# GpSimd's upper part held behind VectorE's last operation of a step, and the second attention's stages one step earlier

## The chip, the cores and the metric

One core of one Trainium2 chip runs the kernel. The metric is the device time of one execution in microseconds, lower is better; the time of a kernel is the median of its runs.

## What is computed

Two set-attention blocks over 12480 tokens of 128 features with 32 inducing points, then two feed-forward blocks of width 2048, all in float32:

```python
def mab(q, kv):
    s = scale * (q @ kv.transpose(0, 2, 1))
    s = s - s.max(-1, keepdims=True)
    a = np.exp(s)
    a /= a.sum(-1, keepdims=True) + 1e-09
    return a @ kv
h = mab(I, x)                        # 32 inducing points look at all tokens
x = mab(x, h)                        # every token looks at the 32 results
h = x @ w_in;  x = (h * np.clip(h + 3.0, 0.0, 6.0) / 6.0) @ w_out      # first block
h = x @ w_in2; x = np.maximum(h, 0.0) ** 2 @ w_out2                    # second block
```

## The kernel before

The first attention (lines 260 to 442) gives 32 x 128 numbers and ends some 43 us into the span. Everything after it is the main loop at the end of the program, which the change touches.

The tokens are cut into 25 chunks of 512 columns, chunk 13 of 192 (`SHORT`). The width 2048 is cut into 8 pieces of two 128-row blocks, so a chunk has 8 steps; step k belongs to chunk c = k // 8, piece p = k % 8, and there are K = 200 steps and a tail of 14. Step k works on layer 1 of piece k and on layer 2 of piece j = k - 11, which belongs to an earlier chunk.

For layer 1, `up1` (L598, two matmuls into a PSUM tile h1) applies the attention's second product and the first weight at once: `m4` holds the inducing results times the weight, so the right operand is the chunk's attention weights `a_t`. `gate1` runs a Relu with bias on ScalarE (L606) and then min and product on VectorE (L607, SBUF and PSUM operands). The gated values g1 are split into two parts for the float32r matmuls: `high1` rounds them (hi1; GpSimd at L618, for a few early steps ScalarE), `low1` takes the rest, g1 - hi1, on VectorE (L626). `down1` (L646, six matmuls into yacc) follows two steps later. At a chunk's last piece yacc is written out as yh on ScalarE (L663) and yl on VectorE (L664); yacc has one buffer, so the next chunk's first down1 has to wait for both.

For layer 2, `up2` (L675, six matmuls), `relu2` and `square2` on ScalarE (L686, L690), `high2` (hi2, L700 on ScalarE) and `low2` (L706 on VectorE, both operands in SBUF) do the same, and `down2` (L646, six matmuls into oacc) follows three steps later; a chunk's oacc is copied by VectorE (L719) and stored. A step thus issues 2 + 6 + 6 + 6 = 20 matmuls. The h tiles of both layers and the scores share three PSUM buffers (pool `hp`).

The attention of the next chunk is spread over steps of the present one: `att_scores` (TensorE, L484) and `att_shift` (VectorE: transpose L504, maximum L507, subtraction L509) at p = 1, `att_exp` (ScalarE, L517) at p = 2, `att_norm` (VectorE: L524, L526, L530, L532 and a transpose back, L550) at p = 3, `att_upper` (ScalarE, ah, L570) at p = 4, `att_spread` at p = 5 (VectorE, al, L577, and 16 transfers of 16 KB from ah and al into a_t on the SP queue, L583). The a_t has two buffers.

What sets the order: until step KM = 24 a scheduler of the framework orders the instructions (there the weights are converted too, L173 to L217, on VectorE, GpSimd and ScalarE). From step 24 on (`tc.manual_schedule()`) each engine runs its instructions in the order in which the program issues them. There VectorE's order in a step is gate, low1 of the step before, low2; `high1` is issued behind the gate.

Of the kernel before, what the change touches and what calls it, by code (L numbers as in the profile page):

```python
# [10 lines left out]
F32 = mybir.dt.float32  # L11
F32R = mybir.dt.float32r
# [9 lines left out]
P = 128  # L22
# [42 lines left out]
L1, L2 = 2, 3  # L65
MIX = (0, 3)
PRE = 26
KM = 24
# [7 lines left out]
def induced_attention_then_two_ffn(  # L76
# [11 lines left out]
    nc = tc.nc  # L88
    NT, D = x.shape
    M = indT.shape[1]  # L90
# [19 lines left out]
    sel = const.tile([P, M], F32, name="sel")  # L110
    blk4 = const.tile([P, J], F32, name="blk4")
    three = const.tile([P, 1], F32, name="three")
    ind = const.tile([P, M], F32, name="ind")
    inds = const.tile([P, M], F32, name="inds")
    ht4 = const.tile([P, J, M], F32, name="ht4")
# [11 lines left out]
    def load_x(c):  # L127
        t = xpool.tile([P, size[c]], F32, tag="xc", name="xc")
        n = at_token[c]
        nc.sync.dma_start(t, xT[:, n:n + size[c]])  # L130
        x_of[c] = t
# [95 lines left out]
    def tick():  # L227
        n = len(ticks)
        ticks.append(n)
        for g in list(live):  # L230
            if next(g, live) is live:
                live.remove(g)
        for item, (when, cut_at, _) in PLAN.items():
            if when == n:
                load_until(item)
                live.append(convert(item))
                next(live[-1])
        for item, (when, cut_at, _) in PLAN.items():
            if cut_at == n:
                live.append(cut(item))  # L240
                next(live[-1])
# [18 lines left out]
    with ExitStack() as pro:  # L260
# [159 lines left out]
        for g in range(NG - 1):  # L420
            j = g % J
# [47 lines left out]
    def mix_low(q):  # L469
        t = m4[2 * M:, q * CW:(q + 1) * CW]  # L470
        nc.vector.tensor_tensor(out=t, in0=mixed.pop(q)[2 * M:, :], in1=t, op=ALU.subtract)
# [4 lines left out]
    def blocks(c):  # L476
        nb = J if size[c] == CH else 2
        return nb, size[c] // nb
# [17 lines left out]
    def att_shift(c):  # L496
        nb, n = blocks(c)
        s = att.pop(c)
        if c == 0:
            st = hp.tile([P, J, M], F32, tag="h", name="pst")  # L500
            nc.tensor.transpose(st.rearrange("p j i -> p (j i)"), s, ident)
        else:
            st = sp.tile([M * nb, n // M, M], F32, tag="st", name="st", bufs=1)
            nc.vector.transpose(st.rearrange("p b i -> p (b i)"), s)  # L504
        shape = list(st.shape)
        nm = sp.tile(shape[:2], F32, tag="nm", name="nm")
        nc.vector.tensor_reduce(out=nm, in_=st, axis=AX.X, op=ALU.max, negate=True)  # L507
        t = sp.tile(shape, F32, tag="t", name="t")
        nc.vector.tensor_tensor(  # L509
            out=t, in0=st, in1=nm.unsqueeze(2).to_broadcast(shape), op=ALU.add  # L510
        )
        att[c] = t

    def att_exp(c):
        t = att.pop(c)
        e = sp.tile(list(t.shape), F32, tag="e", name="e")
        nc.scalar.activation(e, t, AF.Exp, scale=SCALE)  # L517
        att[c] = e

    def att_weights(c):  # L520
        e = att.pop(c)
        shape = list(e.shape)
        l = sp.tile(shape[:2], F32, tag="l", name="l")
        nc.vector.tensor_reduce(out=l, in_=e, axis=AX.X, op=ALU.add)  # L524
        le = sp.tile(shape[:2], F32, tag="le", name="le")
        nc.vector.scalar_tensor_tensor(  # L526
            out=le, in0=l, scalar=EPS, in1=l, op0=ALU.add, op1=ALU.max
        )
        r = sp.tile(shape[:2], F32, tag="r", name="r")
        nc.vector.reciprocal(r, le)  # L530
        a = sp.tile(shape, F32, tag="a", name="a")
        nc.vector.tensor_tensor(  # L532
            out=a, in0=e, in1=r.unsqueeze(2).to_broadcast(shape), op=ALU.mult
        )
        return a

    def att_norm(c):
        a = att_weights(c)
        if c == 0:
            a4 = sp.tile([P, J, 2, 2, M], F32R, tag="a4", name="a4", bufs=1)  # L540
            nc.vector.tensor_copy(a4[:, :, 0, 0, :], a)
            nc.scalar.copy(a4[:, :, 1, 0, :], a)
            for k in range(2):
                last = nc.vector.tensor_tensor(
                    out=a4[:, :, k, 1, :], in0=a, in1=a4[:, :, 0, 0, :], op=ALU.subtract
                )
            att[c] = a4
            return last
        at = sp.tile([a.shape[0], a.shape[1] * M], F32, tag="aback", name="aback", bufs=1)
        nc.vector.transpose(at, a.rearrange("p b i -> p (b i)"))  # L550
        att[c] = at

    def att_turn(c):
        a4 = att.pop(c)
# [8 lines left out]
        return nc.scalar.copy(a_t[c], pt)  # L563


    def att_upper(c):
        nb, n = blocks(c)
        at = att.pop(c)
        ah = sp.tile([M * nb, n], F32R, tag="ah", name="ah", bufs=1)
        nc.scalar.copy(ah, at)  # L570
        att[c] = at, ah

    def att_spread(c):
        nb, n = blocks(c)
        at, ah = att.pop(c)
        al = sp.tile([M * nb, n], F32R, tag="al", name="al", bufs=1)
        nc.vector.tensor_tensor(out=al, in0=at, in1=ah, op=ALU.subtract)  # L577
        a_t[c] = sp.tile([P, size[c]], F32R, tag="at", name="at")
        for v, part in enumerate((ah, al)):
            for u in range(2):  # L580
                for b in range(nb):
                    to = M * (2 * u + v)
                    nc.sync.dma_start(  # L583
                        a_t[c][to:to + M, b * n:(b + 1) * n].bitcast(F32),
                        part[M * b:M * (b + 1), :].bitcast(F32),
                    )

    K = NCH * NP
    h1, g1, hi1, lo1 = {}, {}, {}, {}
# [137 lines left out]
    def on(f, k):  # L727
        if 0 <= k < K:
            f(k)
# [28 lines left out]
    for k in range(K + OFF + L2 + 1):  # L758
        if k == KM:
            behind.close()  # L760
            ctx.enter_context(tc.manual_schedule())
        c, p = divmod(k, NP)
        j = k - OFF
        on(up1, k)
        if k < KM:
            on(low1, k - 1)
        tick()
        on(gate1, k)
        on(high1, k)
        if k >= KM:  # L770
            on(low1, k - 1)
        on(square2, j - 1)
        on(up2, j)
        on(relu2, j)
        on(high2, j - 1)
        on(low2, j - 2)
        tick()
        if k in MIX:
            q = MIX.index(k) + 2
            mix(q)  # L780
            mix_high(q)
            mix_low(q)
        if c + 1 < NCH:
            if p == 0 and LAST < c + 2 < NCH:
                load_x(c + 2)
            if p == 1:
                att_scores(c + 1)
                att_shift(c + 1)
            if p == 2:
                att_exp(c + 1)  # L790
            if p == 3:
                att_norm(c + 1)
            if p == 4:
                att_upper(c + 1)
            if p == 5:
                att_spread(c + 1)
        on(down1, k - L1)
        on(down2, j - L2)


# [26 lines left out]
```

## Time and profile before

| | us |
|---|---|
| median of 3 runs | 1019.51 (1017.94 to 1025.77) |
| the profiled execution, its own time | 1021.25 |
| its span in the trace | 1019.1 |
| busy: TensorE / VectorE / ScalarE / GpSimd | 969.5 / 932.8 / 822.1 / 392.6 |

The span is the time from the first to the last recorded instruction; the execution's own time has 2.15 us around it. PE is TensorE's matmuls, PEld its weight loads, DVE VectorE, ACT ScalarE, POOL GpSimd, SP the engine that issues transfers. The ends of matmuls are modelled, so their starts tell the pace. A bracket behind a row gives the idle time of the engine before it and what ended it.

### The profile page before, as it was taken

Reading aid. Unit: us, or ns where it says so; the run is one execution under the profiler, and the core shown is the slowest. Engines: PE = TensorE matmul, PEld = TensorE weight load, DVE = VectorE, ACT = ScalarE, POOL = GpSimd, SP = SyncE. Lnnn points to the kernel's source line nnn. Section 1 sums busy time; section 2 is a strip of 40 time slices with the busy share of each in tenths; the row PEclk is TensorE's granted clock in tenths of the full one; section 3 lists DMA queues with packets and bytes.
Section 4 is the critical chain, followed back from the end, with each engine's and each line's share of the span. In section 5 each row is a group of like instructions: output and inputs, shape, how many; then the busy total and the mean of one; then the engine's idle time right before and its main releaser. Section 6 shows DMA issues by size and latency. Waiting matters only on the chain.

```text
span 1019.1 us, 12914 instructions
## 1 busy us (share of the span) xinstructions
PE 969.5 (95%) x4614; PEld 764.3 (75%) x4614; DVE 932.8 (92%) x956; ACT 822.1 (81%) x952; POOL 392.6 (39%) x241
## 2 busy tenths in 40 slices
PE   8777999999999999999999879999999999999998
PEld 6434787787787787787788768778778778778786
DVE  4898889999999999999997898999999999999974
ACT  6646898888888888888889757888888888888886
POOL 2465214343343343343451244334334334334323
PEclk9997999999999999999999999999999999999999
DMA  9521010010010010000000010011011011000000
GB/s 354 167 69 50 18 32 6 26 32 6 27 32 5 27 32 6 27 25 5 27 25 9 23 32 25 3 30 32 2 31 29 4 31 31 3 20 21 1 11 21
DMA packets 32879, 34.54 MB, mean 34 GB/s; under 512 B 7600, under 2 KB 25008, under 8 KB 32304
## 3 DMA queue, kind: packets, MB, share of 16 engines
q1 hardware_dynamic: 32816, 33.73, 10.5%
q8 instruction: 36, 0.59, 0.2%
q14 instruction: 27, 0.22, 0.1%
HBM read 21.18 MB, written 6.39 MB: 27 GB/s over the span
## 4 chain that ended last, share of the span: by engine, by line
DVE 58%; PE 27%; ACT 6%; DMA 4%; issue 3%; SPq 1%; POOL 1%; ACTq 0%; DVEq 0%; POOLq 0%
DVE lo L706 22%; DVE g L607 14%; DVE lo L626 13%; PE oacc L646 9%; PE yacc L646 8%; PE h L675 6%; ACT g L606 3%; PE h L598 3%; DMA at<-ah 2%; DVE yl L664 1%; ACT hi L700 1%; SPq L583 1%; ACT g L690 1%; DVE osb L719 1%; DMA raw<-in_w1a 1%
## 5 line engine op out<-in xcount | busy, mean ns | idle before, releaser
L618 POOL TENSOR_SCALAR hi<-g 128x1024 fp32r<-128x1024 f32 (+1 forms) x180 | 330.6, 1837 | 539.4 <-DVE g L607 539.4
L706 DVE TENSOR_TENSOR lo<-g,hi 128x1024 fp32r<-128x1024 f32 (+2 forms) x201 | 380.2, 1892 | 12.3 <-PE oacc L646 6.0
L606 ACT ACTIVATE g<-h,three 128x1024 f32<-128x1024 f32 (+1 forms) x200 | 219.2, 1097 | 143.1 <-PE h L598 142.7
L607 DVE SCALAR_TENSOR_TENSOR g<-g,h 128x1024 f32<-128x1024 f32 (+1 forms) x200 | 236.1, 1182 | 34.8 <-ACT g L606 34.4
L626 DVE TENSOR_TENSOR lo<-g,hi 128x1024 fp32r<-128x1024 f32 (+1 forms) x187 | 221.9, 1187 | 5.1 <-POOL hi L618 3.6
L690 ACT ACTIVATE g<-g 128x1024 f32<-128x1024 f32 (+2 forms) x201 | 206.0, 1026 | 0.4
L686 ACT ACTIVATE g<-h 128x1024 f32<-128x1024 f32 (+2 forms) x201 | 199.5, 993 | 6.8 <-PE h L675 6.7
L700 ACT CAST hi<-g 128x1024 fp32r<-128x1024 f32 (+2 forms) x188 | 191.6, 1020 | 0.0
L675 PE MATMUL h<-yh,wh 128*128 128x512 f32 (+1 forms) x400 | 155.2, 388 | 0.4 <-DVE g L607 0.2
L675 PE MATMUL h<-yh,wl 128*128 128x512 f32 (+1 forms) x400 | 154.3, 386 | 0.0
L675 PE MATMUL h<-yl,wh 128*128 128x512 f32 (+1 forms) x400 | 154.1, 385 | 0.0
L598 PE MATMUL h<-at,m 128*128 128x512 f32 (+1 forms) x400 | 129.7, 407 | 15.8 <-DMA at<-al 7.8
L646 PE MATMUL yacc<-hi,wh 128*128 128x512 f32 (+1 forms) x374 | 118.3, 397 | 18.1 <-DVE yl L664 18.1
L646 PE MATMUL oacc<-hi,wh 128*128 128x512 f32 (+1 forms) x400 | 123.9, 390 | 1.0 <-DVE osb L719 1.0
L646 PE MATMUL oacc<-hi,wl 128*128 128x512 f32 (+1 forms) x400 | 122.1, 386 | 0.0
L646 PE MATMUL oacc<-lo,wh 128*128 128x512 f32 (+1 forms) x400 | 122.0, 386 | 0.0
L646 PE MATMUL yacc<-hi,wl 128*128 128x512 f32 (+1 forms) x374 | 114.3, 387 | 0.0
L646 PE MATMUL yacc<-lo,wh 128*128 128x512 f32 (+1 forms) x374 | 114.0, 386 | 0.0
L598 PEld LDWEIGHTS h<-at,m 128*128 128x128 f32 x400 | 75.5, 193 | 39.3 <-issue 14.3
L646 PEld LDWEIGHTS yacc<-hi,wh 128*128 128x128 f32 x374 | 66.5, 188 | 41.7 <-issue 30.7
L646 PEld LDWEIGHTS oacc<-hi,wh 128*128 128x128 f32 x400 | 73.4, 189 | 22.1 <-issue 6.8
L675 PEld LDWEIGHTS h<-yh,wh 128*128 128x128 f32 x400 | 75.6, 189 | 17.7 <-ACT g L686 1.3
(114 smaller groups left out, 854.8 us busy)
## 6 DMA issues: line engine op xcount, KB each, us to landing
outT<-osb SPq DMA_DIRECT2D x23, 256.0 KB, 2.2
xc<-in_xT SPq DMA_DIRECT2D x22, 256.0 KB, 2.8
xg<-in_xT SPq DMA_DIRECT2D x4, 1024.0 KB, 7.1
at<-ah SPq DMA_DIRECT2D x184, 16.0 KB, 1.8
at<-al SPq DMA_DIRECT2D x184, 16.0 KB, 1.8
raw<-in_w1a SPq DMA_DIRECT2D x4, 512.0 KB, 8.9
raw<-in_w1b SPq DMA_DIRECT2D x4, 512.0 KB, 9.0
raw<-in_w2a SPq DMA_DIRECT2D x4, 512.0 KB, 4.3
```

The source lines that it names most:

```text
L583: nc.sync.dma_start(a_t[c][to:to + M, b * n:(b + 1) * n].bitcast(F32), part[M * b:M * (b + 1), :].bitcast(F32),)
L598: nc.tensor.matmul(h1[k][:, u, :size[c]], lhsT=m4[:, f * P:(f + 1) * P], rhs=a_t[c], start=True, stop=True)
L606: nc.scalar.activation(g1[k], h, AF.Relu, bias=three)
L607: nc.vector.scalar_tensor_tensor(out=g1[k], in0=g1[k], scalar=6.0, in1=h, op0=ALU.min, op1=ALU.mult)
L618: nc.gpsimd.tensor_scalar(out=hi1[k], in0=g1[k], scalar1=1.0, scalar2=1.0, op0=ALU.mult, op1=ALU.mult)
L626: (nc.gpsimd if k in LOW1_P else nc.vector).tensor_tensor(out=lo1[k], in0=g1.pop(k), in1=hi1[k], op=ALU.subtract)
L646: nc.tensor.matmul(acc, lhsT=w[:, f * P:(f + 1) * P], rhs=g[:, u, :], start=(p == 0 and n == 0), stop=(p == NP - 1 and n == 5),)
L675: nc.tensor.matmul(h2[k][:, u, :size[c]], lhsT=w, rhs=y, start=(n == 0), stop=(n == 2))
L686: nc.scalar.activation(g2[k][:, u, :], h[:, u, :n], AF.Relu)
L690: nc.scalar.activation(g2[k][:, u, :], g2[k][:, u, :], AF.Square)
L700: nc.scalar.copy(hi2[k][:, u, :], g2[k][:, u, :])
L706: (nc.gpsimd if k in LOW2_P else nc.vector).tensor_tensor(out=lo2[k][:, u, :], in0=g[:, u, :], in1=hi2[k][:, u, :], op=ALU.subtract)
```

## The change

From step 24 on, `high1(k)` is issued at the end of step k, behind a new copy on GpSimd of one column (128 x 1, L805 of the changed kernel) out of the last tile that VectorE writes in step k: lo1 of the step before, or t, a or al where an attention stage stands behind it. Low1 moves behind low2, and down1 and down2 are issued ahead of the attention's stages instead of behind them. Those move up, in all steps: scores and shift to p = 0, exp to p = 1, norm to p = 2, and spread to p = 3. Spread now also holds the transpose back and the upper part ah, which VectorE makes instead of ScalarE; `att_upper` goes.

```diff
--- before.py
+++ after.py
@@ -110,6 +110,7 @@
     sel = const.tile([P, M], F32, name="sel")
     blk4 = const.tile([P, J], F32, name="blk4")
     three = const.tile([P, 1], F32, name="three")
+    turn = const.tile([P, 1], F32, name="turn")
     ind = const.tile([P, M], F32, name="ind")
     inds = const.tile([P, M], F32, name="inds")
     ht4 = const.tile([P, J, M], F32, name="ht4")
@@ -510,6 +511,7 @@
             out=t, in0=st, in1=nm.unsqueeze(2).to_broadcast(shape), op=ALU.add
         )
         att[c] = t
+        return t[:, 0, :1]
 
     def att_exp(c):
         t = att.pop(c)
@@ -536,6 +538,7 @@
 
     def att_norm(c):
         a = att_weights(c)
+        att[c] = a
         if c == 0:
             a4 = sp.tile([P, J, 2, 2, M], F32R, tag="a4", name="a4", bufs=1)
             nc.vector.tensor_copy(a4[:, :, 0, 0, :], a)
@@ -546,9 +549,7 @@
                 )
             att[c] = a4
             return last
-        at = sp.tile([a.shape[0], a.shape[1] * M], F32, tag="aback", name="aback", bufs=1)
-        nc.vector.transpose(at, a.rearrange("p b i -> p (b i)"))
-        att[c] = at
+        return a[:, 0, :1]
 
     def att_turn(c):
         a4 = att.pop(c)
@@ -563,17 +564,14 @@
         return nc.scalar.copy(a_t[c], pt)
 
 
-    def att_upper(c):
-        nb, n = blocks(c)
-        at = att.pop(c)
-        ah = sp.tile([M * nb, n], F32R, tag="ah", name="ah", bufs=1)
-        nc.scalar.copy(ah, at)
-        att[c] = at, ah
-
     def att_spread(c):
         nb, n = blocks(c)
-        at, ah = att.pop(c)
+        a = att.pop(c)
+        at = sp.tile([M * nb, n], F32, tag="aback", name="aback", bufs=1)
+        nc.vector.transpose(at, a.rearrange("p b i -> p (b i)"))
+        ah = sp.tile([M * nb, n], F32R, tag="ah", name="ah", bufs=1)
         al = sp.tile([M * nb, n], F32R, tag="al", name="al", bufs=1)
+        nc.vector.tensor_copy(ah, at)
         nc.vector.tensor_tensor(out=al, in0=at, in1=ah, op=ALU.subtract)
         a_t[c] = sp.tile([P, size[c]], F32R, tag="at", name="at")
         for v, part in enumerate((ah, al)):
@@ -584,6 +582,7 @@
                         a_t[c][to:to + M, b * n:(b + 1) * n].bitcast(F32),
                         part[M * b:M * (b + 1), :].bitcast(F32),
                     )
+        return al[:, :1].bitcast(F32)
 
     K = NCH * NP
     h1, g1, hi1, lo1 = {}, {}, {}, {}
@@ -766,36 +765,45 @@
             on(low1, k - 1)
         tick()
         on(gate1, k)
-        on(high1, k)
-        if k >= KM:
-            on(low1, k - 1)
+        if k < KM:
+            on(high1, k)
         on(square2, j - 1)
         on(up2, j)
         on(relu2, j)
         on(high2, j - 1)
         on(low2, j - 2)
+        if k >= KM:
+            on(low1, k - 1)
         tick()
         if k in MIX:
             q = MIX.index(k) + 2
             mix(q)
             mix_high(q)
             mix_low(q)
+        if k >= KM:
+            on(down1, k - L1)
+            on(down2, j - L2)
+        behind_it = lo1[k - 1][:, 0, :1].bitcast(F32) if KM <= k < K else None
         if c + 1 < NCH:
             if p == 0 and LAST < c + 2 < NCH:
                 load_x(c + 2)
+            if p == 0:
+                att_scores(c + 1)
+                behind_it = att_shift(c + 1)
             if p == 1:
-                att_scores(c + 1)
-                att_shift(c + 1)
+                att_exp(c + 1)
             if p == 2:
-                att_exp(c + 1)
+                behind_it = att_norm(c + 1)
             if p == 3:
-                att_norm(c + 1)
-            if p == 4:
-                att_upper(c + 1)
-            if p == 5:
-                att_spread(c + 1)
-        on(down1, k - L1)
-        on(down2, j - L2)
+                behind_it = att_spread(c + 1)
+        if k < KM:
+            on(down1, k - L1)
+            on(down2, j - L2)
+        elif k < K:
+
+            n = behind_it.shape[0]
+            nc.gpsimd.tensor_copy(turn[:n], behind_it)
+            high1(k)
 
 
 # ---- launch: one core ----
```

On VectorE, steps 33 and 34 of the kernel before (chunk 4, p = 1 and the start of p = 2; g, lo and hi with numbers are the layers' tiles, L607 the gate, L626 low1, L706 low2):

```order
L607 SCALAR_TENSOR_TENSOR g_1897<-g_1897,h_1894 128x1024
L626 TENSOR_TENSOR lo_1902<-g_1859,hi_1862 128x1024
L706 TENSOR_TENSOR lo_1916<-g_1838,hi_1876 128x1024
L504 STREAM_TRANSPOSE st<-ps 128x128
L507 TENSOR_REDUCE nm<-st 128x4
L509 TENSOR_TENSOR t<-st,nm 128x128
L664 SCALAR_TENSOR_TENSOR yl<-yacc,yh 128x512
L607 SCALAR_TENSOR_TENSOR g_1948<-g_1948,h_1945 128x1024
L626 TENSOR_TENSOR lo_1953<-g_1897,hi_1900 128x1024
L706 TENSOR_TENSOR lo_1967<-g_1874,hi_1914 128x1024
L607 SCALAR_TENSOR_TENSOR g_1987<-g_1987,h_1984 128x1024
```

The same place in the changed kernel, from the gate of step 32 (p = 0) to the gate of step 34 (lines are one or two lower: L606 is the gate, L625 low1, L705 low2):

```order
L606 SCALAR_TENSOR_TENSOR g_1868<-g_1868,h_1865 128x1024
L705 TENSOR_TENSOR lo_1883<-g_1804,hi_1844 128x1024
L625 TENSOR_TENSOR lo_1885<-g_1831,hi_1863 128x1024
L505 STREAM_TRANSPOSE st<-ps 128x128
L508 TENSOR_REDUCE nm<-st 128x4
L510 TENSOR_TENSOR t<-st,nm 128x128
L606 SCALAR_TENSOR_TENSOR g_1918<-g_1918,h_1915 128x1024
L705 TENSOR_TENSOR lo_1933<-g_1842,hi_1881 128x1024
L625 TENSOR_TENSOR lo_1935<-g_1868,hi_1913 128x1024
L663 SCALAR_TENSOR_TENSOR yl<-yacc,yh 128x512
L606 SCALAR_TENSOR_TENSOR g_1961<-g_1961,h_1958 128x1024
```

Low2 now stands ahead of low1, the shift's three operations (st, nm, t) end step 32, and yl comes with only the three large operations of step 33 ahead of it.

On GpSimd, some steps of the kernel before that have nothing but hi1:

```order
L618 TENSOR_SCALAR hi_1789<-g_1786 128x1024
L618 TENSOR_SCALAR hi_1826<-g_1823 128x1024
L618 TENSOR_SCALAR hi_1862<-g_1859 128x1024
L618 TENSOR_SCALAR hi_1900<-g_1897 128x1024
L618 TENSOR_SCALAR hi_1951<-g_1948 128x1024
```

And chunk 4's steps from p = 7 of the chunk before to p = 3 in the changed kernel, where L805 is the copy:

```order
L805 COPY turn<-lo_1848 128x1
L617 TENSOR_SCALAR hi_1863<-g_1831 128x1024
L805 COPY turn<-t 128x1
L617 TENSOR_SCALAR hi_1913<-g_1868 128x1024
L805 COPY turn<-lo_1935 128x1
L617 TENSOR_SCALAR hi_1956<-g_1918 128x1024
L805 COPY turn<-a 128x1
L617 TENSOR_SCALAR hi_2002<-g_1961 128x1024
L805 COPY turn<-al 128x1
L617 TENSOR_SCALAR hi_2062<-g_2007 128x1024
```

Each hi1 now has a copy ahead of it in GpSimd's queue, and what the copy reads names the VectorE operation that it waits for.

## Rows read from the trace of the kernel before

**Rows 1.** The page, part 1: busy us (share) and instructions of each engine.
```profile
PE 969.5 (95%) x4614; PEld 764.3 (75%) x4614; DVE 932.8 (92%) x956; ACT 822.1 (81%) x952; POOL 392.6 (39%) x241
```
**Rows 2.** Groups by line and shape from 160 us: busy us, mean ns | idle before.
```profile
L706 DVE TENSOR_TENSOR lo<-g,hi 128x1024 fp32r<-128x1024 f32 x178 | 350.3, 1968 | 11.6 <-PE oacc L646 6.0 <-ACT hi L700 3.3 <-POOL hi L695 1.9
L626 DVE TENSOR_TENSOR lo<-g,hi 128x1024 fp32r<-128x1024 f32 x167 | 202.6, 1213 | 0.0
L607 DVE SCALAR_TENSOR_TENSOR g<-g,h 128x1024 f32<-128x1024 f32 x166 | 200.4, 1207 | 21.4 <-ACT g L606 21.3
...
L618 POOL TENSOR_SCALAR hi<-g 128x1024 fp32r<-128x1024 f32 x166 | 316.4, 1906 | 475.6 <-DVE g L607 475.6
```
**Rows 3.** Timeline, steps 33 and 34: start us, us, engine, line, operation.
```profile
195.06 0.61 ACT L663 ACTIVATE yh<-yacc 128x512 fp32r<-128x512 f32 x1
...
195.73 0.62 PE L598 MATMUL h<-at,m 128*128 128x512 f32 x2
...
196.38 1.12 ACT L606 ACTIVATE g<-h,three 128x1024 f32<-128x1024 f32 x1 [0.71 <-PE h L598]
...
196.85 0.30 DVE L504 STREAM_TRANSPOSE st<-ps 128x128 f32<-128x128 f32 x1
...
197.72 0.68 DVE L664 SCALAR_TENSOR_TENSOR yl<-yacc,yh 128x512 fp32r<-128x512 f32 x1
198.32 1.21 DVE L607 SCALAR_TENSOR_TENSOR g<-g,h 128x1024 f32<-128x1024 f32 x1
...
198.55 0.70 PE L646 MATMUL yacc<-hi,wh 128*128 128x512 f32 x2 [0.85 <-DVE yl L664]
...
199.45 1.22 DVE L626 TENSOR_TENSOR lo<-g,hi 128x1024 fp32r<-128x1024 f32 x1
...
199.69 1.89 POOL L618 TENSOR_SCALAR hi<-g 128x1024 fp32r<-128x1024 f32 x1 [3.83 <-DVE g L607]
...
200.45 0.62 PE L646 MATMUL oacc<-hi,wl 128*128 128x512 f32 x2
200.58 2.06 DVE L706 TENSOR_TENSOR lo<-g,hi 128x1024 fp32r<-128x1024 f32 x1
...
201.36 0.61 PE L598 MATMUL h<-at,m 128*128 128x512 f32 x2
```
**Rows 4.** Waits of TensorE: us in total, times, longest us.
```profile
PE yacc L646 <- DVE yl L664: 18.1, 21, 2.5
PE h L598 <- DMA at<-al: 7.8, 3, 4.6
```
**Rows 5.** Stretches: length, busy us (x instructions) by engine, granted clock, DMA share, GB/s.
```profile
152.57:529.81 377.24, 369.41 (x1658) 295.68 (x1657) 367.50 (x348) 318.19 (x346) 154.83 (x81) 1.00 0.07 21
529.81:626.55 96.74, 88.75 (x466) 72.79 (x464) 82.44 (x97) 71.07 (x98) 31.20 (x23) 0.96 0.06 18
626.55:973.99 347.44, 340.65 (x1526) 273.17 (x1525) 340.03 (x313) 294.17 (x318) 138.29 (x74) 1.00 0.07 20
```
**Rows 6.** Timeline of VectorE and GpSimd in the early steps, at 65 and 99 us.
```profile
65.63 1.21 DVE L607 SCALAR_TENSOR_TENSOR g<-g,h 128x1024 f32<-128x1024 f32 x1
65.80 0.61 POOL L177 TENSOR_SCALAR cve<-cve 128x512 f32<-128x512 f32 x1 [0.38 <-DVE cve L173]
...
99.23 1.07 POOL L695 TENSOR_SCALAR hi<-g 128x1024 fp32r<-128x1024 f32 x1
```
**Rows 7.** Groups by line of GpSimd's start: its smallest operation.
```profile
L817 POOL MEMSET const-float32-1.0<- 128x1 f32 x1 | 0.1, 100 | 0.0
```
**Rows 8.** Timeline: a step's start, six short matmuls, SP's transfers into a_t.
```profile
190.61 0.62 PE L598 MATMUL h<-at,m 128*128 128x512 f32 x2
...
577.42 0.25 PE L675 MATMUL h<-yh,wh 128*128 128x192 f32 x1
...
578.07 0.66 PE L646 MATMUL yacc<-hi,wh 128*128 128x512 f32 x2
...
593.68 3.75 SPq L583 DMA_DIRECT2D at<-al  x6
```

## The prediction, made before the changed kernel was timed

> **What bounds the kernel now.** I read the busy times first: TensorE 95% and VectorE 92% of the span [rows 1], two engines that could each be the bound. So I went to the pace of TensorE next. In a step without a wait it issues 20 matmuls of 512 columns. From 200.45 to 201.36 it starts four in 0.91 us [rows 3], right after a wait of 0.85 us, so nothing queued up behind held it: 0.2267 us each is its own pace, and a step costs 20 x 0.2267 = 4.53 us. The step from 190.61 to 195.73 is 5.12 us, because the scores of the next chunk stand in it: 0.59 us more [rows 3, 8]. The step from 195.73 to 201.36 is 5.63 us, 1.1 us too long, and the trace says why: yacc waits for VectorE's yl [rows 3]. The list of waits has 21 such waits in the kernel, and three for the transfers into a_t [rows 4].
>
> Then why yl is late. VectorE's three large operations are of the same size, two of them the same operation, yet low1 (L626) and the gate (L607) take 1.21 us, low2 (L706) 1.97 us, and GpSimd's hi (L618) 1.91 us [rows 2], while the same GpSimd operation with little beside it takes 1.07 us [rows 6]. The timeline shows the pairing: low1 starts at 199.45, hi at 199.69 and is recorded until 201.58; low2 starts at 200.58 and is recorded for 2.06 us [rows 3]. If hi runs only once low1 has let go at about 200.6, it ends after 1.07 us of its own, and low2 then needs its 1.2 us: one at a time explains both lengths. Low2 loses 1.97 - 1.21 = 0.76 us in a step, 178 x 0.76 = 135 us from 160 us on. VectorE has just enough time for its 4.53 us steps, and where the attention adds its operations (196.85 to 197.72) yl comes late [rows 3]. So the gap between the pace and the measured stretches is the room that the change can win, and no more: TensorE's pace is the floor.
>
> **The change, part by part.**
>
> GpSimd's wait. From step 24 on, hi1(k) is queued behind a 128x1 copy that reads VectorE's last result of step k (low1(k-1), or the attention's last operation). Hi1 then starts when VectorE goes on to gate(k+1) or idles. Does the gate collide with it? At 65.63 a gate takes 1.21 us while a GpSimd operation on 128x512 takes 0.61 us inside it, from 65.80 [rows 6]; both have their undisturbed lengths. The gate reads one operand from PSUM, the lows both from SBUF. So low2 falls to 1.21 us, and VectorE's three operations to 3 x 1.14 = 3.4 us in a 4.53 us step.
>
> Price of the wait: the copy is not in the trace. From below, GpSimd's memset of 128x1 takes 0.10 us [rows 7]; from above, its 128x512 operation 0.61 us [rows 6]; a 128x1 copy is nearer the memset, and I take 0.10, plus 0.2 us until GpSimd starts after its releaser (as 199.69 stands after 199.45). Hi1 ends 0.1 + 0.2 + 1.07 = 1.4 us after low1(k-1). VectorE's next operation, the gate, takes 1.13 of these, so at worst 0.25 us of low2 is held when VectorE has no idle time, at the upper bound 0.75 us. Its step would be 3.7 to 4.2 us, still under 4.53: hidden by TensorE. Behind hi1 on GpSimd nothing waits but the next copy; who waits for hi1(k) is low1(k), now the last of VectorE's step k+1, two operations later, and then down1(k) in step k+2. The new order (low2 before low1) delays lo1 by one operation, so its reader in step k+2 needs a look. Take step k at time 0. Relu1 starts at 0.65 and lasts 1.12 [rows 3], gate 1.8 to 2.9, low2 to 4.1, low1(k-1) to 5.2, hi1(k) to 6.6. In step k+1 (4.53 later) the gate is at 6.3 to 7.5, low1(k) ends at 9.8. Down1(k) starts at 9.06 + 8 x 0.2267 = 10.9. One microsecond to spare.
>
> The yl. In the step with the chunk's last down1 (p = 1) yh on ScalarE starts 4.45 us into the step (195.06 against 190.61) and ends at 5.06 [rows 3, 8]. VectorE has ended low1 at 5.2 and has no attention in front of yl any more, since scores and shift moved to p = 0; yl takes 0.68, to 5.9. The next yacc wants to start at 4.53 + 1.81 = 6.34. The wait of 1.1 us goes, with 0.4 us to spare. What is late next is TensorE itself.
>
> The attention's stages. Scores and shift move from p = 1 to p = 0, behind down1 and down2 of the step; exp, norm and spread to p = 1, 2, 3. The 0.59 us of scores stay on TensorE. On VectorE the cast ah is added (bounds: none, and 0.30 us as the transpose of the same tile [rows 3]; it stands in p = 3, which has a microsecond of room) and ScalarE loses it. The 16 transfers into a_t are issued one by one on SP, six in 3.75 us [rows 8], 16 in 10 us: now all after p = 3 rather than eight after p = 4 and eight after p = 5. They end two steps earlier, and the three waits for them [rows 4] go, two of which stand in the short chunk's stretch. Output and x transfers keep their place behind them on SP with over a step of slack.
>
> **The sum**, made against the profiled execution (1021.25 us, span 1019.1), by the stretches of [rows 5], cut at steps 25, 104, 126 and 199:
> - 152.57 to 529.81, 79 steps: 79 x 4.53 + 10 x 0.59 = 364 us instead of 377.24: 13.2.
> - 626.55 to 973.99, 73 steps: 73 x 4.53 + 8 x 0.59 = 335.6 instead of 347.44: 11.8.
> - 529.81 to 626.55, the 22 steps around the 192-token chunk: 280 matmuls of 512 columns x 0.2267 = 63.5; 160 of 192 columns, six of which start in 578.07 - 577.42 = 0.65 us [rows 8], 0.108 each = 17.3; scores 3 x 0.59 = 1.8; together 82.6. I add 2.7 for changes between widths and one yl that a 3.25 us step cannot hide: 85.3 instead of 96.74: 11.4.
> - Before 148 us the order of the first 24 steps is made by a scheduler and changes in many places. The longest wait for a_t, 4.6 us [rows 4], can go, and as much can be lost between the weights' conversions: between -5 and +5, and I take 0. The last 45 us hold no changed operation that waits.
>
> Together 36.4 us: 984.9 for that execution, which stands 1.7 above the median of 1019.51: 983 us.
>
> The floor of 0.2267 us is measured at a granted clock of 1.00, the 2.4 GHz level [rows 3, 5]. The Trainium skill speaks against it: by its page "TensorE: Matmul & The Clock Gate", section "Wait — 56ns, not 53.3ns?", warm matmuls of 512 columns start every 215.7 ns, by which a step would be 4.31 us and the sum 983 - 165 x 0.22 = 947, an estimate. The trace does not agree with that figure, and the measured pace decides; that TensorE is quicker is a rival below, priced from rows.
>
> **Rivals.**
>
> *TensorE is quicker than its pace shows* (2%). For it: VectorE is busy 97% of the two long stretches [rows 5], so 4.53 us could be VectorE's pace. Against: four starts in 0.91 us after a wait, while nothing is asked of VectorE. The time would lie between ScalarE's busy time, 822 us [rows 1], and 983; the middle is 903.
>
> *The wait for yl stays* (11%). For it: only 0.4 us of slack, and ScalarE's yh is the last of five operations in its queue. Then 19 chunks keep 1.1 us and the short chunk's stretch 3.5: 24.4 us less gain, 1007.
>
> *The copy holds nothing back* (4%). If hi1 started without regard to the copy before it, the collisions would stay and only the moved stages would help: a_t's waits in the short stretch (3) and part of yl's (0.9 x 19 / 2), 1008. By the skill's "GPSIMD Engine Reference", section "2.1 Instruction dispatch", a Pool instruction's completion does not hold back the next one; no run shows such a pair here. Against it: hi1 is behind the copy in one queue, and it is the copy's start that waits.
>
> *Gate and hi1 exclude each other* (4%), the case on the slower side. Then low1, copy, hi1, gate and low2 are one chain: 3.4 + 0.2 + 0.1 + 1.07 = 4.8 us a step, over TensorE's 4.53 in some 165 steps: 983 + 165 x 0.27 = 1028; with the copy at 0.61, 5.3 us and 1110. It decides once the copy and the start together pass 0.06 us. For it: two lows show the exclusion plainly. Against: 1.21 us at 65.63, and 0.61 beside it.
>
> **How the numbers follow.** My forecast has 75%, with a range of its own of 976 to 993 (5 either way for the first 24 steps, and some leftover waits above). The yl case and the idle copy, 15%, end near 1007; a mixture of them, a part of the waits kept, lies under that. Another 4% I give to unforeseen waits that leave the time near 1015. The range that holds 8 in 10 is 975 to 1004. A measurement of this kernel tells about 1% from no change. Faster by over 1% (under 1009.3): 0.75 + 0.02 + most of the 15% = 0.90. Within 1%: 0.06. Slower: 0.04.
>
> **What would show it.** Right: L706 and L618 near 1.2 and 1.1 us in the lines; steps of 4.53 us, chunks of 36.9; no PE yacc wait for yl, no wait for a_t after 148 us; VectorE's busy share near 80%; hi beside gates in the timeline. Wrong: gates over 1.3 us (exclusion), steps longer than 4.6 us with TensorE waiting for lo1 or hi1, yl still named as releaser, or an early stretch that ends later than 148 us.

## The result and the profile after

The changed kernel took 988.18 us (median of 4 runs, 985.48 to 990.42), the kernel before 1019.69 (4 runs). The ratio is 0.9684, 95% interval 0.9643 to 0.9725: faster by 3.2%. The forecast was 983.0 with a range of 975 to 1004. The profiled execution of the changed kernel took 988.34 us, span 986.5.

The page, part 1 and the first line of part 4, to be held against [rows 1]:

```profile
PE 958.1 (97%) x4614; PEld 766.4 (78%) x4614; DVE 810.9 (82%) x980; ACT 816.5 (83%) x928; POOL 274.1 (28%) x417
...
PE 89%; DVE 6%; ACT 2%; DMA 1%; POOL 1%; issue 1%; SPq 0%; DVEq 0%; POOLq 0%
```

And the first line of part 4 on the page before:

```profile
DVE 58%; PE 27%; ACT 6%; DMA 4%; issue 3%; SPq 1%; POOL 1%; ACTq 0%; DVEq 0%; POOLq 0%
```

VectorE has 122 us less to do and GpSimd 119 us less, though both run more instructions. Part 4 is the chain of work that ended last, by engine: it was 58% VectorE and 27% TensorE before; now TensorE has 89% of it.

Groups by line and shape of the changed kernel from 155 us on (busy us, mean ns | idle before), against [rows 2]:

```profile
L705 DVE TENSOR_TENSOR lo<-g,hi 128x1024 fp32r<-128x1024 f32 x180 | 221.1, 1228 | 11.3 <-PE oacc L645 6.0 <-ACT hi L699 3.3 <-POOL hi L694 1.9
L625 DVE TENSOR_TENSOR lo<-g,hi 128x1024 fp32r<-128x1024 f32 x169 | 205.7, 1217 | 1.1 <-POOL hi L617 1.1
L606 DVE SCALAR_TENSOR_TENSOR g<-g,h 128x1024 f32<-128x1024 f32 x167 | 203.8, 1221 | 102.5 <-ACT g L605 99.8
...
L617 POOL TENSOR_SCALAR hi<-g 128x1024 fp32r<-128x1024 f32 x168 | 177.2, 1055 | 0.3 <-issue 0.3
...
L805 POOL COPY turn<-lo 128x1 f32<-128x1 f32 x113 | 21.6, 191 | 337.9 <-DVE lo L625 337.9
```

Low2 (now L705) fell from 1968 to 1228 ns, hi1 (L617) from 1906 to 1055, and the gate (L606), which now runs beside hi1, rose only from 1207 to 1221. VectorE, which had 21 us of idle time in front of its gates, has 102 us. The last row is the new wait: GpSimd's copy waits for low1.

Timeline of the changed kernel, part of steps 34 and 35, the same place as [rows 3]:

```profile
197.30 1.22 DVE L625 TENSOR_TENSOR lo<-g,hi 128x1024 fp32r<-128x1024 f32 x1
...
197.68 0.60 ACT L662 ACTIVATE yh<-yacc 128x512 fp32r<-128x512 f32 x1
197.78 0.61 PE L597 MATMUL h<-at,m 128*128 128x512 f32 x2
...
198.44 0.68 DVE L663 SCALAR_TENSOR_TENSOR yl<-yacc,yh 128x512 fp32r<-128x512 f32 x1
...
198.58 0.18 POOL L805 COPY turn<-lo 128x1 f32<-128x1 f32 x1 [2.97 <-DVE lo L625]
...
198.72 1.05 POOL L617 TENSOR_SCALAR hi<-g 128x1024 fp32r<-128x1024 f32 x1
...
199.59 0.62 PE L645 MATMUL yacc<-hi,wh 128*128 128x512 f32 x2
199.64 1.22 DVE L606 SCALAR_TENSOR_TENSOR g<-g,h 128x1024 f32<-128x1024 f32 x1 [0.52 <-ACT g L605]
...
202.31 0.62 PE L597 MATMUL h<-at,m 128*128 128x512 f32 x2
...
204.12 1.22 DVE L606 SCALAR_TENSOR_TENSOR g<-g,h 128x1024 f32<-128x1024 f32 x1
...
204.34 1.05 POOL L617 TENSOR_SCALAR hi<-g 128x1024 fp32r<-128x1024 f32 x1
205.26 1.22 DVE L705 TENSOR_TENSOR lo<-g,hi 128x1024 fp32r<-128x1024 f32 x1
```

The copy starts 0.06 us after low1's recorded end, hi1 0.14 later. At 204.34 hi1 starts inside a gate and runs beside it but for its last 0.05 us, and both have their own lengths. Yl ends at 199.12 and the next yacc starts at 199.59 without a wait. From 197.78 to 202.31 a step takes 4.53 us.

The stretches of the changed kernel, cut at the same steps (25, 104, 126, 199) as [rows 5], and the time before the first step (columns as there):

```profile
156.26:519.74 363.48, 363.48 (x1652) 297.45 (x1649) 311.61 (x358) 316.23 (x336) 94.46 (x158) 1.00 0.08 22
519.74:605.72 85.98, 84.79 (x465) 70.84 (x464) 70.67 (x101) 69.99 (x95) 21.93 (x44) 1.00 0.08 21
605.72:941.43 335.71, 335.71 (x1526) 274.78 (x1525) 285.65 (x320) 292.63 (x310) 87.36 (x146) 1.00 0.07 20
0.00:45.10 45.10, 39.49 (x449) 28.35 (x449) 25.56 (x65) 26.03 (x63) 12.00 (x18) 0.92 0.77 277
```

And of the kernel before, the time before its first step:

```profile
0.00:43.54 43.54, 36.73 (x448) 26.65 (x448) 25.26 (x64) 25.98 (x63) 12.03 (x18) 1.00 0.80 287
```

In both long stretches TensorE is recorded as busy for every microsecond, so taking away more waits cannot make them shorter. What was lost lies ahead of them: step 25 starts at 156.26 us instead of 152.57.

### The profile page after: what moved, and what is told of

It reads as the page before. It is cut to its first block, busy times and chain, and to the rows that moved or that the text cites. A ratio compares the mean times of both kernels' runs of the same rounds, so it can differ in the third digit from the quotient of the medians.

```text
span 986.5 us, 12958 instructions
## 1 busy us (share of the span) xinstructions
PE 958.1 (97%) x4614; PEld 766.4 (78%) x4614; DVE 810.9 (82%) x980; ACT 816.5 (83%) x928; POOL 274.1 (28%) x417
## 4 chain that ended last, share of the span: by engine, by line
PE 89%; DVE 6%; ACT 2%; DMA 1%; POOL 1%; issue 1%; SPq 0%; DVEq 0%; POOLq 0%
PE oacc L645 26%; PE h L674 26%; PE yacc L645 25%; PE h L597 9%; DVE g L606 1%; DMA raw<-in_w1a 1%; PE ps L485 1%; DVE cve L189 1%; DVE cve L185 1%; DMA xg<-in_xT 1%; PE yacc L633 1%; ACT g L605 1%; PE xt L336 0%; POOL cve L178 0%; POOL wl L218 0%
## 5 line engine op out<-in xcount | busy, mean ns | idle before, releaser
L606 DVE SCALAR_TENSOR_TENSOR g<-g,h 128x1024 f32<-128x1024 f32 (+1 forms) x200 | 238.4, 1193 | 112.9 <-ACT g L605 109.9
L705 DVE TENSOR_TENSOR lo<-g,hi 128x1024 fp32r<-128x1024 f32 (+2 forms) x201 | 241.1, 1200 | 16.4 <-PE oacc L645 10.4
L625 DVE TENSOR_TENSOR lo<-g,hi 128x1024 fp32r<-128x1024 f32 (+1 forms) x187 | 222.3, 1189 | 2.3 <-POOL hi L617 2.3
L617 POOL TENSOR_SCALAR hi<-g 128x1024 fp32r<-128x1024 f32 (+1 forms) x180 | 185.5, 1030 | 30.5 <-ACT g L685 16.4
L645 PE MATMUL yacc<-hi,wh 128*128 128x512 f32 (+1 forms) x374 | 114.2, 387 | 3.7 <-DVE yl L663 3.7
L805 POOL COPY turn<-lo 128x1 f32<-128x1 f32 x113 | 21.6, 191 | 337.9 <-DVE lo L625 337.9
L597 PEld LDWEIGHTS h<-at,m 128*128 128x128 f32 x400 | 72.9, 189 | 34.0 <-issue 10.1
L674 PEld LDWEIGHTS h<-yl,wh 128*128 128x128 f32 x400 | 75.2, 188 | 15.3
```

What stands on the lines that cost most here:

```text
L597: nc.tensor.matmul(h1[k][:, u, :size[c]], lhsT=m4[:, f * P:(f + 1) * P], rhs=a_t[c], start=True, stop=True)
L606: nc.vector.scalar_tensor_tensor(out=g1[k], in0=g1[k], scalar=6.0, in1=h, op0=ALU.min, op1=ALU.mult)
L617: nc.gpsimd.tensor_scalar(out=hi1[k], in0=g1[k], scalar1=1.0, scalar2=1.0, op0=ALU.mult, op1=ALU.mult)
L625: (nc.gpsimd if k in LOW1_P else nc.vector).tensor_tensor(out=lo1[k], in0=g1.pop(k), in1=hi1[k], op=ALU.subtract)
L645: nc.tensor.matmul(acc, lhsT=w[:, f * P:(f + 1) * P], rhs=g[:, u, :], start=(p == 0 and n == 0), stop=(p == NP - 1 and n == 5),)
L674: nc.tensor.matmul(h2[k][:, u, :size[c]], lhsT=w, rhs=y, start=(n == 0), stop=(n == 2))
```

## The experiments

Three parts of the span tell the kernels apart, from the start of step 0, of step 25 and the span's end: the start, where nothing was changed, steps 0 to 24, whose order a scheduler makes, and the rest, whose order is the program's. In us, from the timeline of each run:

| kernel | start | steps 0 to 24 | step 25 to the end | median, us | ratio to before (95%) |
|---|---|---|---|---|---|
| before | 43.54 | 109.03 | 866.5 | 1019.69 | |
| changed | 45.10 | 111.16 | 830.2 | 988.18 | 0.9684 (0.9643 to 0.9725) |
| e1_wait_only | 43.64 | 108.36 | 835.8 | 990.42 | 0.9709 (0.9688 to 0.9729) |
| e2_stages_only | 44.55 | 111.22 | 854.5 | 1013.55 | 0.9935 (0.9914 to 0.9957) |
| e3_old_early | 44.92 | 108.67 | 829.9 | 985.73 | 0.9662 (0.9644 to 0.9680) |
| e4_changed_again | 44.56 | 111.22 | 830.0 | 987.98 | 0.9691 (0.9660 to 0.9721) |
| e5_extra_3 | 44.36 | 111.12 | 924.9 | 1080.62 | 1.0598 (1.0574 to 1.0621) |
| e6_extra_1 | 47.01 | 111.29 | 831.1 | 989.36 | 0.9702 (0.9677 to 0.9728) |
| e7_low1_first | 43.58 | 111.53 | 830.3 | 987.81 | 0.9693 (0.9676 to 0.9710) |
| e8_old_in_chunks_1_2 | 43.52 | 108.03 | 830.0 | 983.03 | 0.9640 (0.9624 to 0.9656) |
| e9_old_in_chunk_2 | 44.12 | 110.84 | 830.3 | 987.37 | 0.9678 (0.9654 to 0.9703) |
| e10_old_12_again | 43.60 | 108.16 | 830.1 | 984.54 | 0.9649 (0.9627 to 0.9670) |

Theory A in the expectations is the prediction's mechanism; the other letters are its rivals there, C and D about the loss in the early order.

**e1_wait_only** keeps the wait and puts the attention's stages back to p = 1 to 5, ahead of down1 and down2.

```diff
-        if k >= KM:
-            on(down1, k - L1)
-            on(down2, j - L2)
...
-            if p == 0:
+            if p == 1:
                 att_scores(c + 1)
                 behind_it = att_shift(c + 1)
-            if p == 1:
+            if p == 2:
                 att_exp(c + 1)
...
+        on(down1, k - L1)
+        on(down2, j - L2)
```

> The copy that holds hi1 back stays, from step 24 on, and low2 before low1; the attention's stages, the upper part on ScalarE and the place of down1 and down2 are again those of before. Theory A (the collision of hi1 with the lows was the whole loss; the stages' places matter only before step 24): low2 and low1 take 1.2 us, all stretches from step 25 on as in the changed kernel within 2 us, and the first 24 steps as before, so 984 to 986 us. Theory B (yl has to stand ahead of the shift): the wait of yacc for yl stays in 21 chunks, 0.5 to 1.1 us each, so 995 to 1007 us.

Measured: 990.42 us, between the two, nearer to A. From step 25 on the wait alone gains 866.5 - 835.8 = 30.7 of the 36.3 us. The two long stretches take 364.80 and 336.51 us, 1.3 and 0.8 more than in the changed kernel; the short chunk's takes 89.41, 3.4 more. TensorE's waits of that kernel from 500 to 640 us:

```profile
PE h L620 <- DMA at<-al: 2.5, 2, 1.3
PE yacc L668 <- DVE yl L686: 1.2, 1, 1.2
```

So the wait takes nearly all waits for yl away by itself. What the moved stages add after step 25, 5.6 us, is for the most part (3.4) the short chunk's stretch. The two waits there for the transfers into a_t, 2.5 us, are not in the changed kernel; the wait for yl is in both (1.2 and 0.9 us). Of the 1.3 us in the first long stretch, 0.45 is no gain: with the stages at p = 0, the scores of the first chunk behind step 24 stand in step 24 (4.98 us instead of 4.53), ahead of the cut.

**e2_stages_only** moves the stages and low1 as the change does, and issues hi1 right behind the gate, without a copy.

```diff
-        if k < KM:
-            on(high1, k)
+        on(high1, k)
...
-        elif k < K:
-
-            n = behind_it.shape[0]
-            nc.gpsimd.tensor_copy(turn[:n], behind_it)
-            high1(k)
```

> Hi1 is issued right behind the gate as before, without the copy; all the moved stages and the new order of low2 and low1 stay. Theory A: one of the two lows again takes about 2.0 us and hi1 1.9 us, VectorE needs 8 x 4.25 + 3.9 = 37.9 us a chunk, over TensorE's 36.9, so 1005 to 1014 us. Theory B (the stages' places bring the gain): lows collide, but TensorE does not wait, 985 to 992 us.

Measured: 1013.55 us, as A expected. Groups of this kernel from 155 us on, and below them one of TensorE's waits:

```profile
L625 DVE TENSOR_TENSOR lo<-g,hi 128x1024 fp32r<-128x1024 f32 x169 | 344.4, 2038 | 0.0
L617 POOL TENSOR_SCALAR hi<-g 128x1024 fp32r<-128x1024 f32 x168 | 316.1, 1881 | 477.9 <-DVE g L606 477.9
L705 DVE TENSOR_TENSOR lo<-g,hi 128x1024 fp32r<-128x1024 f32 x179 | 217.3, 1214 | 10.1 <-PE oacc L645 4.5 <-ACT hi L699 3.3 <-POOL hi L694 1.9
```

```profile
PE yacc L645 <- DVE yl L663: 15.5, 20, 2.2
```

In this kernel low2 is the first of the two lows and low1 the second: now low1 takes 2038 ns and low2 1214. The long operation is whichever low comes second, and not one line or one buffer. Yl is waited for 20 times again. The stages without the wait bring 12.0 us after step 25, half of it (6.0) in the short chunk's stretch. Wait and stages each alone, 30.7 + 12.0, are more than the two together, 36.3. That both take from the same waits for yl (18.1 us in 21 before, 1.2 in e1, 15.5 in e2) is the likely reason; how much each wait is worth was not measured. Hi1 issued at the end of the step without the copy was not tried; in most steps nothing but hi1 stands in GpSimd's queue, so its place there alone gives it nothing to wait behind.

**e5_extra_3** and **e6_extra_1** price a later hi1: three or one GpSimd operations on 128x256, whose results nobody reads, stand between copy and hi1.

```diff
             nc.gpsimd.tensor_copy(turn[:n], behind_it)
+            for i in range(3):
+                nc.gpsimd.tensor_scalar(
+                    out=idle, in0=m4[:, :256].bitcast(F32), scalar1=1.0, scalar2=1.0,
+                    op0=ALU.mult, op1=ALU.mult,
+                )
             high1(k)
```

(e6 has `range(1)`.)

> The changed kernel with three more GpSimd operations of 128x256 behind the copy, ahead of hi1; they do nothing that is used. Theory A (low1, copy, hi1, low2 and the next low1 are one chain, which TensorE's 4.53 us still cover): from the changed kernel hi1 ends 1.25 us after low1, the two lows take 2.27 us, the extra ones an estimated 0.37 each, so a link of 4.63 us, with the attention's 2.7 us of small operations 39.7 us a chunk over TensorE's 36.9: some 60 us more, 1035 to 1060 us, with low2 held for over a microsecond. Rival (GpSimd is off the path, busy 28%): 986 to 990 us.

> The same with one such operation. Theory A: a link of 3.9 us, 34 us a chunk, under TensorE's 36.9: 986 to 990 us as the changed kernel, though low2 is held in some steps. Rival (any delay of hi1 costs): 0.37 us in 170 steps, some 60 us more.

Measured for one extra operation: 989.36 us, as A expected; from step 25 on it costs 0.9 us in all (831.1 against 830.2). Groups of e6 from 155 us on, VectorE and GpSimd:

```profile
L706 DVE TENSOR_TENSOR lo<-g,hi 128x1024 fp32r<-128x1024 f32 x180 | 238.3, 1324 | 11.2 <-PE oacc L646 6.0 <-ACT hi L700 3.3 <-POOL hi L695 1.9
...
L808 POOL TENSOR_SCALAR idle<-m 128x256 fp32r<-128x256 f32 x176 | 71.2, 404 | 0.0
```

Hi1 starts 0.4 us later, low2 is held 0.1 us (1324 against 1228 ns), and TensorE hardly notices. Measured for three: 1080.62 us, slower than before, as A said, but 20 us beyond its upper end. Timeline of e5, VectorE and GpSimd, from one low1 (L626) to the next and the one after it:

```profile
191.81 1.22 DVE L626 TENSOR_TENSOR lo<-g,hi 128x1024 fp32r<-128x1024 f32 x1 [1.32 <-POOL hi L618]
...
193.10 0.19 POOL L806 COPY turn<-lo 128x1 f32<-128x1 f32 x1 [1.32 <-DVE lo L626]
193.24 2.33 POOL L808 TENSOR_SCALAR idle<-m 128x256 fp32r<-128x256 f32 x3
194.08 1.22 DVE L706 TENSOR_TENSOR lo<-g,hi 128x1024 fp32r<-128x1024 f32 x1
195.53 1.06 POOL L618 TENSOR_SCALAR hi<-g 128x1024 fp32r<-128x1024 f32 x1
196.62 1.23 DVE L626 TENSOR_TENSOR lo<-g,hi 128x1024 fp32r<-128x1024 f32 x1 [1.32 <-POOL hi L618]
...
202.30 1.23 DVE L626 TENSOR_TENSOR lo<-g,hi 128x1024 fp32r<-128x1024 f32 x1 [1.31 <-POOL hi L618]
```

The three take 2.33 us, of which low2 covers 1.1: this time GpSimd is the one that is held. Hi1 ends at 196.6, low1 waits 1.32 us for it, and the next copy waits for low1: a ring of copy, extra operations, low2, hi1 and low1 of 196.62 - 191.81 = 4.81 us, over TensorE's 4.53. In the steps with the attention's VectorE operations these stand in the ring as well, 202.30 - 196.62 = 5.68 us. With three such steps of eight that is 5.14 a step, which is what the 79 steps from 25 to 104 take in this kernel: 406.1 / 79. This is the place on the slower side of the change. It decides between 0.4 and 2.3 us of delay, and the change itself stays short of it. A's price was too low, with a link of 4.63 us for the 4.81: it counted the extra operations at 0.37 us each, and they took 0.62 in the mean, with low2 between them.

**e7_low1_first** puts low1 ahead of low2 again, and the copy reads low2's result.

```diff
-        on(low2, j - 2)
         if k >= KM:
             on(low1, k - 1)
+        on(low2, j - 2)
...
-        behind_it = lo1[k - 1][:, 0, :1].bitcast(F32) if KM <= k < K else None
+        behind_it = lo2[j - 2][:, 0, :1].bitcast(F32) if KM <= k < K else None
```

> The changed kernel with low1 ahead of low2 again from step 24 on, and the copy reading low2's result. Theory A: low1 comes 1.1 us earlier and may wait up to 0.3 us for hi1 where VectorE has no idle time; TensorE covers it, 986 to 990 us. Rival (the order of the lows is what gives hi1 its time): low1 waits for hi1 in most steps and yl comes late again, 992 to 1000 us.

Measured: 987.81 us, and 830.3 from step 25 on, as the changed kernel. Low1 now waits for hi1 23 times in this kernel's list from 155 us on, 0.3 us in the mean, where the changed kernel has 1.1 us of it in all; these waits stay hidden under TensorE:

```profile
DVE lo L625 <- POOL hi L617: 7.1, 23, 1.4
```

So the order of the two lows, which the change turned round too, carries none of the gain.

**e3_old_early, e8, e9 and e10** ask where the 2.1 us in steps 0 to 24 went. They are the changed kernel with the attention's stages at their old places in some early steps: in e3 those of k < KM, in e8 and e10 (the same kernel, run again) those with c = 1 and 2, which are steps 8 to 23, in e9 those with c = 2, steps 16 to 23. **e4_changed_again** is the changed kernel without an edit, beside e1 to e3 on one chip.

```diff
-            if p == 0:
-                att_scores(c + 1)
-                behind_it = att_shift(c + 1)
...
+            if c in (1, 2):
+                if p == 1:
+                    att_scores(c + 1)
+                    behind_it = att_shift(c + 1)
...
+                if p == 5:
+                    behind_it = att_spread_old(c + 1)
+            else:
+                if p == 0:
+                    att_scores(c + 1)
+                    behind_it = att_shift(c + 1)
```

> The changed kernel, with the stages of the attention for chunks 1 to 3 (issued in steps 0 to 23) at their old places. Theory C (the 3.7 us by which step 25 comes later than before are the scheduler's new order of the first 24 steps, above all yl behind the norm in step 17): step 25 starts at 152 to 153.5 us and the time is 983 to 985.5 us. Rival (it is a matter of the execution, such as the granted clock of the first 43 us, 0.92 against 1.00): 987 to 989 us, as the changed kernel.

> The changed kernel itself, beside the others on the same chip. Both theories: 985 to 990.5 us, as its four runs so far.

> The changed kernel with the old places of the stages in steps 8 to 23 only (chunks 1 and 2), the new ones in steps 0 to 7. In the trace of the changed kernel step 11 starts 3.3 us earlier than before, and all of that and 3.7 us more is lost from step 13 to step 18. Theory C (the loss is made by the stages among the scheduler's steps 8 to 23): step 25 starts at 149 to 152 us, time 981 to 984 us. Rival (what is won early is lost to the weights' conversions in any order): step 25 at 153 to 156 us, 985 to 988 us.

> The changed kernel with the old places of the stages in steps 16 to 23 only (chunk 2). From the first to the 25th step the changed kernel takes 111.2 us, the one with the old places in chunks 1 and 2 took 108.0, the kernel before 109.0. Theory D (the wait for yl in step 18, 2.8 us and a half clock behind it, is the whole loss): 107 to 108.5 us, time 982 to 984 us. Rival (the waits of 1.2 us in steps 13 and 15, from chunk 1's stages, are lost too): 109 to 110.5 us, 984.5 to 987 us.

> The kernel with the old places in chunks 1 and 2 again, beside the one before. Both: 982 to 984 us, 108.0 us from the first to the 25th step.

Measured: e3 and e8 give the loss back, 108.67 and 108.03 us instead of 111.16 (e3's step 25 at 153.59 and its time of 985.73 are 0.1 and 0.2 outside what C had named, with a start 1.4 us later than in the kernel before). E9 does not, 110.84 us and 987.37, a little beyond its rival's ranges too; but its edit did not take the wait for yl away, as the rows below show, so it does not test theory D. E10 repeats e8's 108.0 with 108.16; its median of 984.54 is 0.5 above what was expected. In the changed kernel step 18 takes 9.17 us, 4.84 in the kernel before. Timeline of the changed kernel, VectorE, GpSimd and TensorE around it:

```profile
119.80 1.05 POOL L617 TENSOR_SCALAR hi<-g 128x1024 fp32r<-128x1024 f32 x1 [3.77 <-DVE g L606]
119.95 0.91 DVE L528 SCALAR_TENSOR_TENSOR le<-l 128x4 f32<-128x4 f32 x1
...
120.82 1.05 POOL L694 TENSOR_SCALAR hi<-g 128x1024 fp32r<-128x1024 f32 x1
121.11 0.89 DVE L534 TENSOR_TENSOR a<-e,r 128x128 f32<-128x128 f32 x1
...
122.27 1.18 DVE L625 TENSOR_TENSOR lo<-g,hi 128x1024 fp32r<-128x1024 f32 x1
123.38 0.68 DVE L663 SCALAR_TENSOR_TENSOR yl<-yacc,yh 128x512 fp32r<-128x512 f32 x1
...
124.20 1.19 PE L645 MATMUL yacc<-hi,wh 128*128 128x512 f32 x2 [2.79 <-DVE yl L663]
125.19 1.05 PE L645 MATMUL yacc<-hi,wl 128*128 128x512 f32 x2
126.05 1.05 PE L645 MATMUL yacc<-lo,wh 128*128 128x512 f32 x2
```

The scheduler has put the whole norm and low1 in front of yl, and in these steps nothing holds hi1 back: le takes 0.91 us and a 0.89 beside GpSimd's two hi, where the same operations take 0.16 and 0.29 at 203 us. TensorE waits 2.79 us, and behind the wait two matmuls take 0.86 us from start to start instead of 0.45: the 1.2 GHz level, until 127.7 (granted clock 0.51 from 124.20 to 127.70). The same wait, 2.8 us, is in the traces of e2 and e4 to e7, and not in those of e1, e3, e8 and e10. In e8 yl stands ahead of low1 (timeline of e8, VectorE and TensorE):

```profile
120.23 0.68 DVE L686 SCALAR_TENSOR_TENSOR yl<-yacc,yh 128x512 fp32r<-128x512 f32 x1
120.83 1.48 DVE L648 TENSOR_TENSOR lo<-g,hi 128x1024 fp32r<-128x1024 f32 x1
...
121.06 0.70 PE L668 MATMUL yacc<-hi,wh 128*128 128x512 f32 x2
```

and in e9 behind it, with a low1 of 2.06 us:

```profile
120.07 2.06 DVE L648 TENSOR_TENSOR lo<-g,hi 128x1024 fp32r<-128x1024 f32 x1
122.05 0.68 DVE L686 SCALAR_TENSOR_TENSOR yl<-yacc,yh 128x512 fp32r<-128x512 f32 x1
...
122.88 0.70 PE L668 MATMUL yacc<-hi,wh 128*128 128x512 f32 x2 [1.99 <-DVE yl L686]
```

Both have the stages of steps 16 to 23 at their old places. What differs is steps 8 to 15, and with them the scheduler's order further on. Over all kernels the length of steps 0 to 24 goes with this wait: 111.1 to 111.5 us with 2.8 us of it, 110.84 with 1.99, 108.0 to 109.0 without. Step 18 takes 9.17, 8.37 (e9) and 4.69 us (e8); these 4.5 us are more than the whole difference of 3.1 between the changed kernel and e8. So the loss is an order in which yl comes late in step 18, which is what theory D named; it hangs on the places of the stages in steps 8 to 15, and not on those in steps 16 to 23, but by which of the scheduler's rules was not tried.

With the old places in steps 8 to 23 the kernel is the quickest of all: 983.03 and 984.54 us (8 runs, 982.8 to 985.4), where the changed kernel had 987.98 and 988.18 (985.5 to 991.5). Steps 0 to 24 are 3.0 to 3.1 us shorter in its traces; most of the rest that its profiled executions gain, 1.5 to 1.6 us, is an earlier start, which the edit doesn't touch.

## Why the prediction was right, and where it was off

**The exclusion, right.** "One at a time explains both lengths", said the prediction: hi1 fell to 1.055 us and low2 to 1.228 (forecast 1.07 and 1.21), and e2 shows the other half, the length going over to low1 as soon as that is second. This is also what the Trainium skill says in "SBUF — State Buffer", section "SBUF: two separate sides": a VectorE operation with two SBUF inputs and a GpSimd operation that reads SBUF hold their shared ports for the whole instruction, whichever starts first, and the other blocks fully. The trace agrees in both directions, 2038 and 1881 ns in e2, and the small le at 119.95 that needs 0.91 us.

**The copy, mis-sized and harmless.** It took 0.19 us, not 0.10. The start behind its releaser was shorter than the 0.2 taken, so hi1 ends 1.25 us after low1 (198.52 to 199.77) and not 1.4. E6 shows that another 0.4 would have been hidden too, as the prediction's bound of 0.61 had it.

**The floor, right.** 79 steps were forecast at 364 us and took 363.48; 73 at 335.6 and took 335.71; the short stretch at 85.3 and took 85.98. Together the three stretches gave 36.25 us of the 36.4; 0.45 of it is the scores that moved ahead of the cut, so that the first stretch has nine sets of them and not the ten of the forecast. The 2.7 us added for the short stretch came from no row; over the 82.6 of its matmuls it took 3.4 more. The rival that TensorE is quicker than its pace shows is settled: TensorE was busy all of 363.48 us with VectorE at 311.61, and the steps still cost 4.53. By the Trainium skill, "TensorE: Matmul & The Clock Gate", section "Wait — 56ns, not 53.3ns?", the estimate had been 947 us from 215.7 ns a matmul; the trace does not agree, it stays at 226.7 ns at a granted clock of 1.00.

**The wait for yl, right in its size, though less of it is the stages' doing.** The slack was forecast as 0.4 us and is 0.47 (199.12 to 199.59). The prediction took the earlier shift as what clears yl's way; e1 shows that the quicker lows clear it by themselves in the whole chunks (long stretches 2.1 us longer in all). The slack does not hold in the short chunk: one wait for yl of 0.9 us is left there, of the 21 with 18.1 us [rows 4].

**The waits for a_t, right after step 25.** None is left there, and e1, with the stages at their old places, has two of them with 2.5 us. The rival that the copy holds nothing back fell with the copy's 337.9 us of waiting for low1, behind which hi1 starts 0.14 us after the copy does, and the rival that gate and hi1 exclude each other with the gate's 1221 ns.

**The step that failed: "I take 0" for the first 24 steps.** Measured by that execution, step 25 starts 3.69 us later than before; that the early stretch ends later was one of the prediction's own signs of being wrong (step 24 starts at 151.27 us instead of 148.04). Of these 1.56 lie before the first step, where the change alters nothing: the granted clock was 0.92 there instead of 1.00, and over all the runs this start varies from 43.5 to 47.0 us (43.5 to 44.6 where the clock was 1.00). The other 2.1 are steps 0 to 24 (111.16 against 109.03), the same in five further runs with the new places (111.1 to 111.5): 0.45 for the scores in step 24, which step 25 no longer has, and 1.7 for the order. That the wait for a_t of 4.6 us [rows 4] can go was right in part, it fell to 1.9; what ate it and more is a wait for yl that the kernel before did not have in these steps, 2.79 us and the half clock behind it. The bounds of -5 to +5 held it, the value did not. For the profiled execution the forecast was 984.9; 3.69 of later start, 0.15 of gain less than forecast and 0.35 less in the tail and outside the span make the measured 988.34 within 0.1. The median lies 1.7 us further off than that, mostly since the execution of the kernel before stood 1.7 us above its median and that of the changed kernel only 0.2.

## What to carry to other kernels

Two engines whose long operations exclude each other show it as one operation with two lengths in the groups; look for the pairing in the timeline, and give the second engine its turn behind the first one's last such operation, beside one that doesn't collide. The turn costs a copy of a single column (0.19 us here), as long as the ring of both engines stays shorter than the step of the engine that bounds. Where a scheduler makes the order, price an earlier stage by what it is put in front of: that part is not computed by hand, and old places can be kept there.

## What the runs showed that was not expected

- GpSimd's order with VectorE is settled operation by operation: of three short GpSimd operations in a row the second and third had low2 between them (2.33 us for the three in e5, 0.40 for one in e6).
- A wait of TensorE can cost more than its length: behind 2.79 us idle the granted clock fell to the 1.2 GHz level, and the eight matmuls after it took 3.49 us, from 124.20 to 127.69, where eight take 8 x 0.2267 = 1.81 at the 2.4 GHz level. The wait of 0.85 us [rows 3] had no such tail. Of waits near 2 us some had one and some had none: the clock fell behind 1.99 us in e9 (0.53 from 124.7 to 127.0), and not behind 2.22 us in e2 at 606.0.
- The kernel before had such a tail too, in the short chunk's stretch, which the prediction did not price by itself. It is part of the 10.8 us that this stretch gained (granted clock 0.96 in [rows 5], 1.00 in the changed kernel). TensorE at that place, and the stretch behind it, columns as in [rows 5]:

```profile
609.86 1.19 PE L646 MATMUL yacc<-hi,wh 128*128 128x512 f32 x2 [2.48 <-DVE yl L664]
```

```profile
609.86:616.25 6.39, 6.39 (x18) 5.28 (x19) 3.54 (x4) 1.25 (x2) 1.88 (x1) 0.52 0.01 3
```

These 18 matmuls, 12 of 512 columns and 6 of 192, would take 12 x 0.2267 + 6 x 0.108 = 3.4 us at the full clock, an estimate from the starts in [rows 3, 8]: some 3 us went with the clock.
